# First half of the first batch in plain f32: the weights' fp16 halves made after it, in one row of tiles

## The chip, the cores and the metric

The kernel runs on one core of one Trainium2 chip. The metric is the device time of one execution in microseconds (us); the figure compared is the median of several runs. Before the change it is 1115.94 us, the median of three runs from 1112.94 to 1116.92.

The core has five engines that run their own instruction streams in order and wait for each other by semaphores: TensorE (PE in the profile, with its weight loads as PEld), VectorE (DVE), ScalarE (ACT), GpSimd (POOL) and SyncE (SP), which here only issues DMAs.

## The reference

There are 8 batches, 8 heads, 576 positions and a head width of 64. Each head is a causal attention with a decay, and its output feeds a feed-forward network (FFN) of width 2048:

```
scores = q @ k.T / sqrt(64)
cum    = cumsum(max(s, 0))
scores = where(causal, scores + min(-(cum[i] - cum[j]), 0), -1e9)
x      = softmax(scores) @ v                 # 8 heads side by side: 4608 x 512
h      = x @ w_in                            # 512 x 2048, given in float64
g      = where(h >= 1, h, where(h <= -1, 0, (h + 1)**2 / 4))
y      = g @ w_out                           # 2048 x 512, given in float64
```

The kernel computes g as min(relu(h/2 + 1/2), 1) * max(h, relu(h/2 + 1/2)), with scales by powers of two drawn in.

## The kernel before, in words

**Jobs.** The attention works in jobs: one pair of heads of one batch, and one half of its positions. The first half of a batch has 320 positions (three tiles of rows), the second 256 (two tiles, against all 576 keys). The list `jobs` runs batch by batch, first the first half of all four pairs, then the second half. A job has eight slots (`att_slot`): slots 2 to 7 hold its score units. For each unit PE makes the scores, DVE adds the mask and takes the row minimum (L418), ACT takes the exponential (L429), and POOL, ACT and DVE make fp16 halves of the normalised weights (L450 to L456). A DMA transposes these (L457). Slot 7 of the next job multiplies by V into the tile `px` (L475, `att_out`), and from `px` the job's part of X is made: a high fp16 half on ACT (L486) and a low one on DVE (L487). The first eight jobs (0 to 7, the first batch) make their scores by plain f32 matmuls (L407, tiles QF and KF), all later ones by two fp32r matmuls (L412, L413).

**FFN.** Each half batch is one FFN round of 16 steps `ft`, each for 128 of the 2048 hidden values. `ffn_h` multiplies 4 tiles of X by 128 columns of `w_in`: three fp16 products for each (high by high, high by low, low by high), so 12 matmuls for a step. ACT (L542) and DVE (L545, L546) make g in f32, and `g_split` makes its two fp16 halves on ACT (L556) and POOL (L557). `ffn_y` adds the step's share to four outputs (`m` 0 to 3) in four banks of the accumulator memory (PSUM), 3 matmuls each, so 12 again.

**Weights.** The weights arrive as float64 words, in 16 chunks of 512 KB each for `w_in` (tile `wir`) and for `w_out` (tile `wor`). `Weights.decode` makes f32 of a chunk with ACT (L198, L211) and DVE (L199, L212 to L215), and PE sums its size for a bound (L203). `Weights.scale` makes a scale from the bounds of a group of chunks. `Weights.split` then makes the fp16 halves: the high one on ACT (L228), the low one either in one DVE instruction (L236) or as a scaling (POOL L231 for `w_in`, ACT L233 for `w_out`) and a POOL subtraction (L234). For `w_in`, 11 of the 16 chunks take the DVE way, 5 the POOL way; for `w_out` all take the POOL way.

**Tiles.** 16 tiles `WI` hold the halves of `w_in`; 18 tiles `WO` first hold the f32 values of `w_in`, then the f32 values of `w_out` (two tiles further on) and then its halves. So a chunk of `w_out` can be decoded only where the chunk of `w_in` that lay there has been split.

**Order.** Jobs 0 to 3 come first, with the decoding of `w_in` between their slots; then `a_in` (a bound over all of `w_in`), `batch_scales(0)` (a dozen small DVE instructions), the first three loads of `w_out` (which wait for `a_in`) and all 16 splits of `w_in`. Then the loop over `j` begins. In `j` 0 to 15 each turn has one step of `ffn_h` for the first round and two of the tasks that decode and split `w_out`; in `j` 16 to 31 it has two steps of `ffn_y` for two of the four outputs. In these 32 turns 40 attention slots are placed, that is, jobs 4 to 8. From `j` 32 on every FFN step takes two turns, and `ffn_y` runs two steps behind `ffn_h`.

A planner then sorts the instructions of each engine. It takes them by priority (their place in the program, moved forward where `tc.high_priority` says so: `TTR_LEAD`, `FFN_LEAD`, `X_LEAD`, `W2_LEAD`) as they become ready on its own model of time. The order on each engine is fixed before the kernel runs, and on the chip each engine keeps it.

Of the kernel before, what the change touches and what calls it, by code (L numbers as in the profile page):

```python
# [22 lines left out]
P = 128  # L23
# [31 lines left out]
POOL_LO = {'wi': (8, 12, 13, 14, 15), 'wo': range(16)}  # L55
POOL_SCALE = ('wi',)
# [15 lines left out]
def attention_ffn(ctx: ExitStack, tc: tile.TileContext, qT, kT, vT, s, w_in, w_out, yT):  # L72
# [95 lines left out]
    class Weights:  # L168
        def __init__(self, name, src, held, out, tags, order, groups):
            self.name, self.src, self.held, self.out, self.tags = name, src, held, out, tags  # L170
            self.order, self.size = order, NW // groups
            self.group = {c: n // self.size for n, c in enumerate(order)}
# [18 lines left out]
        def decode(self, n):  # L191
            c, g = self.order[n], n // self.size
            raw = self.raw.pop(c)
            w = flat32(self.held[c])
            wi = w.bitcast(I32)
            lw, hw = raw[:, :, 0], raw[:, :, 1]

            A.activation(w, hw.bitcast(F32), AF.Copy, scale=2.0 ** -112)  # L198
            V.tensor_scalar(wi, wi, 3, None, ALU.logical_shift_left)  # L199

            if n % self.size == 0:
                self.sums[g] = ps_y.tile([P, 512], F32, tag=f"y{g}", name=f"sum_{self.name}{g}")
            T.matmul(  # L203
                self.sums[g][:, :NC], ones, w.bitcast(BF16).rearrange("p (n t) -> p n t", t=2)[:, :, 1],
                start=(n % self.size == 0), stop=(n % self.size == self.size - 1),
            )

            if n in self.act_low:
                dst = raw.bitcast(U16).rearrange("p n (t f) -> p n t f", f=4)[:, :, 0, 2]
                src = raw.bitcast(U8).rearrange("p n (t f) -> p n t f", f=8)[:, :, 0, 3]  # L210
                A.activation(dst, src, AF.Identity, bias=floor_bias, scale=2.0 ** -5)  # L211
# [12 lines left out]
        def split(self, n):  # L224
            c, g = self.order[n], n // self.size
            r = self.r[:, g:g + 1]
            w, hi, lo = flat32(self.held[c]), self.out[c][:, 0], self.out[c][:, 1]
            A.activation(hi, w, AF.Copy, scale=r)  # L228
            if n in self.pool_lo:
                if self.name in POOL_SCALE:  # L230
                    G.tensor_scalar(w, w, r, 1.0, ALU.mult, ALU.mult)  # L231
                else:
                    A.activation(w, w, AF.Copy, scale=r)  # L233
# [6 lines left out]
        WO, WI, ((gp, "g", G_BUFS),), [n % 4 * 4 + n // 4 for n in range(NW)], 4,  # L240
# [4 lines left out]
        WO[WO_LAG:], WO, ((ap, "raw", 2), (gp, "x0", 2), (ap, "raw", 2)), list(range(NW)), 2,  # L245
# [218 lines left out]
    def att_out(n, hf):  # L464
# [58 lines left out]
    def ffn_h(b, hf, ft):  # L523
# [4 lines left out]
        for kt in range(NKT):  # L528
            for wl, xl in ((0, 0), (0, 1), (1, 0)):
                T.matmul(  # L530
                    h[:, :N], WI[4 * kt + ft // 4][:, wl, ft % 4 * P:(ft % 4 + 1) * P], x[:, kt, xl],
# [18 lines left out]
    to_split = []  # L550

# [9 lines left out]
    def ffn_y(b, hf, ft, g, ms=tuple(range(NKT))):  # L561
# [4 lines left out]
        for m in ms:  # L566
            c0 = ft % 2 * 2 * P + m % 2 * P
            for n, (wl, gl) in enumerate(((0, 0), (1, 0), (0, 1))):
                T.matmul(  # L569
                    ys[b, hf, m][:, :N], WO[8 * (m // 2) + ft // 2][:, wl, c0:c0 + P], g[:, gl],  # L570
# [31 lines left out]
    for j in range(NPAIR):  # L602
        for k in range(8):
# [19 lines left out]
    def w2_tasks():  # L623
        for g in range(2):
            for c in range(8 * g, 8 * g + 8):
                w2.decode(c)
                w2.load(c + 3)
                yield
            w2.scale(g, TINY)
            batch_y(0, (g,))  # L630
            for c in range(8 * g, 8 * g + 8):
                w2.split(c)
                yield

    t = 8 * NPAIR
    tasks = w2_tasks()
    for j in range(16 * NP):
# [7 lines left out]
        with tc.high_priority(offset=W2_LEAD):  # L645
            for _ in range(W2_RATE):
                next(tasks, None)
        if j >= 2 * NFT:
            ffn_step(j // 2, j % 2)
        elif j < NFT:  # L650
            ffn_step(j, 0)
        else:
            if j == NFT:
                with tc.high_priority(offset=FFN_LEAD):
                    g_split()
            m = 2 * (j // 8 % 2)
            for i in range(j % 8 * 2, j % 8 * 2 + 2):
                ffn_y(*ffn_q[i], ms=(m, m + 1))
            if j == 2 * NFT - 1:
                del ffn_q[:NFT]  # L660
# [32 lines left out]
```

## Time and profile before

| | |
|---|---|
| median of three runs | 1115.94 us |
| the profiled execution: its time | 1111.73 us |
| the profiled execution: its span | 1109.9 us |
| PE busy in the span | 1010.8 us (91%) |
| DVE busy | 846.3 us (76%) |
| ACT busy | 725.8 us (65%) |
| POOL busy | 679.0 us (61%) |

All rows of the trace come from that one execution, and their times count from the span's start. Its time is 1.8 us more than its span. A row of the timeline gives start, duration (us), engine, line, operation, output and inputs, the count of merged instructions, and in brackets how long the engine had been idle before and for whom it waited. A row of the groups gives line, engine, operation, shapes and count, then busy us and mean ns of one, then the idle time before them with what ended it. A row of the windows gives a stretch, its length, then for PE, PEld, DVE, ACT and POOL the busy us with the count of instructions, and at the end the clock that was granted to TensorE (1.00 is full), the busy share of the DMA engines and GB/s. A plain f32 matmul of the program is two records in the trace (x2), each with a weight load of its own.

### The profile page before, as it was taken

Reading aid. Unit: us, or ns where it says so; the run is one execution under the profiler, and the core shown is the slowest. Engines: PE = TensorE matmul, PEld = TensorE weight load, DVE = VectorE, ACT = ScalarE, POOL = GpSimd, SP = SyncE. Lnnn points to the kernel's source line nnn. Section 1 sums busy time; section 2 is a strip of 40 time slices with the busy share of each in tenths; the row PEclk is TensorE's granted clock in tenths of the full one; section 3 lists DMA queues with packets and bytes.
Section 4 is the critical chain, followed back from the end, with each engine's and each line's share of the span. In section 5 each row is a group of like instructions: output and inputs, shape, how many; then the busy total and the mean of one; then the engine's idle time right before and its main releaser. Section 6 shows DMA issues by size and latency. Waiting matters only on the chain.

```text
span 1109.9 us, 25082 instructions
## 1 busy us (share of the span) xinstructions
PE 1010.8 (91%) x8495; PEld 774.9 (70%) x8496; DVE 846.3 (76%) x2325; ACT 725.8 (65%) x1703; POOL 679.0 (61%) x1173
## 2 busy tenths in 40 slices
PE   2456898799999999999999999899999999899998
PEld 1232466587768877777778877687778877787787
DVE  7887966688787877787778877787777887887533
ACT  4765985677567774867567765777576765777432
POOL 4782795775556764766467664666476665765522
PEclk9955999799999999999999999999999999999999
DMA  7876653786468663886468763877387763676300
GB/s 235 218 200 192 170 87 91 158 173 155 100 122 188 148 152 71 187 162 158 79 146 177 161 136 81 177 160 163 68 176 155 165 137 74 158 156 138 68 25 19
DMA packets 340775, 155.01 MB, mean 140 GB/s; under 512 B 290856, under 2 KB 322472, under 8 KB 340648
## 3 DMA queue, kind: packets, MB, share of 16 engines
q1 hardware_dynamic: 330944, 143.49, 59.6%
q10 hardware_dynamic: 9704, 9.93, 2.9%
q8 instruction: 67, 1.10, 0.4%
q14 instruction: 60, 0.49, 0.1%
HBM read 72.31 MB, written 9.73 MB: 74 GB/s over the span
## 4 chain that ended last, share of the span: by engine, by line
PE 61%; DVE 12%; POOL 8%; DMA 7%; issue 6%; ACT 5%; ACTq 0%; SPq 0%; DVEq 0%; POOLq 0%
PE y L569 25%; PE h L530 25%; PE px L475 4%; DMA pt<-pb 3%; PE s L412 3%; PE s L413 3%; DVE pb L456 2%; ACT u L542 2%; POOL pb L453 2%; POOL pb L450 2%; DVE p L418 1%; DVE Q L357 1%; DMA vt<-vb 1%; POOL vb L371 1%; DVE h L545 1%
## 5 line engine op out<-in xcount | busy, mean ns | idle before, releaser
L530 PE MATMUL h<-x,WI 128*128 128x256 f16 (+1 forms) x3072 | 463.9, 290 | 7.4 <-ACT x L486 3.4
L569 PE MATMUL y<-g,WO 128*128 128x256 f16 (+1 forms) x3072 | 457.8, 288 | 7.0 <-POOL g L557 5.3
L530 PEld LDWEIGHTS <-WI 128*128 128x128 f16 x3072 | 291.1, 99 | 97.0 <-issue 13.9
L569 PEld LDWEIGHTS <-WO 128*128 128x128 f16 x3072 | 288.1, 98 | 92.9 <-issue 13.8
L557 POOL TENSOR_TENSOR g<-u,g 128x320 f16<-128x320 f32 (+1 forms) x256 | 206.0, 805 | 152.1 <-ACT g L556 151.6
L429 ACT ACTIVATE p<-p,mn 64x64 f32<-64x64 f32 (+4 forms) x320 | 179.4, 561 | 142.7 <-DVE mn L418 122.2
L542 ACT ACTIVATE u<-h,ub,us 128x320 f32<-128x320 f32 (+1 forms) x256 | 149.1, 583 | 120.3 <-PE h L530 115.3
L545 DVE SCALAR_TENSOR_TENSOR h<-h,ws,u 128x320 f32<-128x320 f32 (+1 forms) x256 | 132.4, 517 | 110.6 <-ACT u L542 108.1
L450 POOL TENSOR_SCALAR pb<-p,rs 64x128 f16<-64x128 f32 (+4 forms) x160 | 95.3, 596 | 171.2 <-DVE rs L446 112.1
L453 POOL TENSOR_TENSOR pb<-p,pb 64x128 f16<-64x128 f32 (+4 forms) x160 | 173.9, 1087 | 9.5
L456 DVE SCALAR_TENSOR_TENSOR pb<-p,rs,pb 64x128 f16<-64x128 f32 (+4 forms) x160 | 134.6, 841 | 47.1 <-POOL pb L450 47.0
L418 DVE CUSTOM_DVE_ANT_0 p<-s,mask 64x64 f32<-64x64 f32 (+4 forms) x320 | 134.4, 420 | 31.3 <-PE s L413 23.0
L412 PE MATMUL s<-K,Q 128*64 128x64 f32 (+1 forms) x336 | 126.2, 377 | 16.0 <-DVE mn L418 10.9
L546 DVE SCALAR_TENSOR_TENSOR u<-u,r,h 128x320 f32<-128x320 f32 (+1 forms) x256 | 130.3, 509 | 6.8 <-DVE h L545 0.5
L451 ACT ACTIVATE p<-p,rs 64x64 f32<-64x64 f32 (+4 forms) x160 | 89.6, 560 | 51.3 <-DVE rs L446 49.4
L556 ACT CAST g<-u 128x320 f16<-128x320 f32 (+1 forms) x256 | 107.9, 421 | 10.3 <-DVE u L546 10.3
L413 PE MATMUL s<-K,Q 68*64 68x64 f32 (+1 forms) x336 | 102.8, 307 | 2.1 <-DMA K<-cumd 1.3
L452 POOL TENSOR_SCALAR pb<-p 64x128 f16<-64x128 f32 (+4 forms) x160 | 93.2, 583 | 11.9 <-ACT p L451 11.0
L475 PEld LDWEIGHTS <-vt 128*64 128x64 f16 x1536 | 73.4, 113 | 36.7 <-issue 30.2
L475 PE MATMUL px<-pt,vt 128*64 128x256 f16 (+3 forms) x1536 | 83.5, 259 | 13.3 <-DMA pt<-pb 8.7
L412 PEld LDWEIGHTS s<-K,Q 128*64 128x64 f32 (+1 forms) x336 | 61.5, 183 | 27.3 <-DVE mn L418 8.2
L413 PEld LDWEIGHTS s<-K,Q 68*64 68x64 f32 (+1 forms) x336 | 61.9, 184 | 5.8 <-issue 1.7
(105 smaller groups left out, 983.0 us busy)
## 6 DMA issues: line engine op xcount, KB each, us to landing
rk<-in_k_dram SPq DMA_DIRECT2D x56, 288.0 KB
v<-in_v_dram SPq DMA_DIRECT2D x32, 288.0 KB
rq<-in_q_dram SPq DMA_DIRECT2D x56, 160.0 KB
rk<-in_k_dram SPq DMA_DIRECT2D x56, 160.0 KB
wir<-in_moe_w_in_dram SPq DMA_DIRECT2D x16, 512.0 KB
wor<-in_moe_w_out_dram SPq DMA_DIRECT2D x16, 512.0 KB
rq<-in_q_dram SPq DMA_DIRECT2D x56, 128.0 KB
out_dram<-o ACTq DMA_DIRECT2D x32, 160.0 KB
```

The lines of the kernel that those rows point to most:

```text
L412: T.matmul(sc[:R, :c1 - c0], Q1[:, hd, qo:qo + R], K1[:, hd, c0:c1], start=True, stop=False)
L413: T.matmul(sc[:R, :c1 - c0], Q2[:KC, hd, qo:qo + R], K2[:KC, hd, c0:c1], start=False, stop=True)
L418: ttr[0] = V.tensor_tensor_reduce(out=Pt[:R, c0:c1], in0=sc[:R, :c1 - c0], in1=mask[:R, mo:mo + c1 - c0], scale=-0.125 if j < F32_JOBS els ...
L429: A.activation(Pt[:R, :W], Pt[:R, :W], AF.Exp, bias=m2[:R], scale=-1.0, accum_out=sums[n, i][:R, hd:hd + 1])
L453: G.tensor_tensor(los[1], pw, his[1], ALU.subtract)
L456: V.scalar_tensor_tensor(los[0], pv, rs[:R, :1], his[0], ALU.mult, ALU.subtract)
L475: T.matmul(px[hd * D:(hd + 1) * D, lo:N], VT[:, vl * NB + j, hd * D:(hd + 1) * D], PT[:, 4 * j + 2 * hd + pl, lo:], start=(m == 0), stop=( ...
L530: T.matmul(h[:, :N], WI[4 * kt + ft // 4][:, wl, ft % 4 * P:(ft % 4 + 1) * P], x[:, kt, xl], start=(n == 0), stop=(n == 3 * NKT - 1),)
L542: first = A.activation(u, h[:, :N], AF.Relu, bias=ubi[b], scale=usc[b][:, fg:fg + 1]).ins
L545: V.scalar_tensor_tensor(h[:, :N], h[:, :N], wsc[b][:, fg:fg + 1], u, ALU.mult, ALU.max)
L557: G.tensor_tensor(g[:, 1], u, g[:, 0], ALU.subtract)
L569: T.matmul(ys[b, hf, m][:, :N], WO[8 * (m // 2) + ft // 2][:, wl, c0:c0 + P], g[:, gl], start=(ft == 0 and n == 0), stop=(ft == NFT - 1 an ...
```

## The change

The first FFN round (batch 0, first half) no longer uses fp16 halves. Its X is one f32 tile (`att_out` makes it by one ACT instruction for each pair), `first_h` multiplies it by the decoded f32 values of `w_in` in plain f32 (4 matmuls for a step instead of 12), g stays in f32 (no `g_split`), and `first_y` multiplies it by the decoded f32 values of `w_out` (one matmul for each output and step instead of 3). Its scales (`us32`, `ws32`) come from the batch's scale of V alone, not from the weights' bounds; its output is copied without a scale.

All weights lie in one row of 34 tiles `WT`: the f32 values of chunk n lie two tiles behind its halves, and those of `w_out` follow those of `w_in`. So `w_out` can be decoded before `w_in` is split, and a split overwrites f32 values which the first round has used. The splits of `w_in` move from ahead of the loop to `j` 4 to 19, one for each turn; those of `w_out` to `j` 24 to 31 (chunks 0 to 7) and, with `W2_LEAD`, two for each turn in `j` 32 to 35. All of `w_out` is decoded in `j` 0 to 7. All 16 low halves of `w_in` are now made by an ACT scaling (the line of L233) and a POOL subtraction (L234); L231 and, for the weights, L236 are no longer used. `a_in`, `batch_scales(0)` and `batch_y(0)` move to `j` 16, and the first loads of `w_out` wait for the last group's bound instead of `a_in`. The 40 attention slots of these turns stay where they were.

```diff
-POOL_LO = {'wi': (8, 12, 13, 14, 15), 'wo': range(16)}
-POOL_SCALE = ('wi',)
+POOL_LO = {'wi': range(16), 'wo': range(16)}
...
-    WI = [cp.tile([P, 2, NC], F16, name=f"WI{c}") for c in range(NW)]
-    WO = [cp.tile([P, 2, NC], F16, name=f"WO{c}") for c in range(NW + WO_LAG)]
+    WT = [cp.tile([P, 2, NC], F16, name=f"WT{c}") for c in range(2 * NW + W_LAG)]
...
+            self.out, self.held = WT[base:base + NW], WT[base + W_LAG:base + W_LAG + NW]
...
             if n in self.pool_lo:
-                if self.name in POOL_SCALE:
-                    G.tensor_scalar(w, w, r, 1.0, ALU.mult, ALU.mult)
-                else:
-                    A.activation(w, w, AF.Copy, scale=r)
+                A.activation(w, w, AF.Copy, scale=r)
                 G.tensor_tensor(lo, w, hi, ALU.subtract)
...
+        if (b, hf) == (0, 0):
+            if p == 0:
+                X[b, hf] = gp.tile([P, NKT, N], F32, tag=f"x{hf}", bufs=2, name=f"x{b}_{hf}")
+            with tc.high_priority(offset=X_LEAD):
+                A.activation(X[b, hf][:, p], px[:, :N], AF.Copy, scale=e)
+            return
...
+    def first_h(ft):
+        N = HALF[0][1]
+        h = ps_h.tile([P, 512], F32, tag="h", name=f"h0_0_{ft}")
+        for kt in range(NKT):
+            T.matmul(
+                h[:, :N], flat32(w1.held[ft // 4 * NKT + kt])[:, ft % 4 * P:(ft % 4 + 1) * P], X[0, 0][:, kt],
+                start=(kt == 0), stop=(kt == NKT - 1),
+            )
+        if ft % 4 == 0:
+            g32.append(gp.tile([P, 4, N], F32, tag="g", bufs=G_BUFS, name=f"g0_0_{ft}"))
+        with tc.high_priority(offset=FFN_LEAD):
+            u = gp.tile([P, N], F32, tag="u", bufs=4, name=f"u0_0_{ft}")
+            A.activation(u, h[:, :N], AF.Relu, bias=half_bias, scale=us32)
+            V.scalar_tensor_tensor(h[:, :N], h[:, :N], ws32, u, ALU.mult, ALU.max)
+            V.scalar_tensor_tensor(g32[-1][:, ft % 4], u, 1.0, h[:, :N], ALU.min, ALU.mult)
+
+    def first_y(ft, ms):
...
+            T.matmul(
+                ys[0, 0, m][:, :N], flat32(w2.held[8 * (m // 2) + ft // 2])[:, c0:c0 + P], g32[ft // 4][:, ft % 4],
+                start=(ft == 0), stop=(ft == NFT - 1),
+            )
...
-    V.tensor_reduce(a_in, w1.bound, axis=AX, op=ALU.max)
-    batch_scales(0)
     for c in range(3):
-        w2.load(c, a_in)
-    for n in range(NW):
-        w1.split(n)
+        w2.load(c, w1.bound[:, 3:4])
     att_out(*jobs[NPAIR - 1])
...
+        if j < NW // 2:
+            with tc.high_priority(offset=W2_LEAD):
+                for c in (2 * j, 2 * j + 1):
+                    w2.decode(c)
+                    w2.load(c + 3)
+                    if c % 8 == 7:
+                        w2.scale(c // 8, TINY)
+        if j < NFT:
+            first_h(j)
+        elif j < 2 * NFT:
+            i = j - NFT
+            if i < 8:
+                for ft in (2 * i, 2 * i + 1):
+                    first_y(ft, (0, 1))
+            else:
+                for ft in range(i % 4 * 4, i % 4 * 4 + 4):
+                    first_y(ft, (i // 4,))
+        if j == NFT:
+            V.tensor_reduce(a_in, w1.bound, axis=AX, op=ALU.max)
+            batch_scales(0)
+            batch_y(0)
+        if 4 <= j < NW + 4:
+            w1.split(j - 4)
+        if NW + 8 <= j < 2 * NW:
+            w2.split(j - NW - 8)
+        elif 2 * NW <= j < 2 * NW + 4:
+            with tc.high_priority(offset=W2_LEAD):
+                for c in (8, 9):
+                    w2.split(c + (j - 2 * NW) * 2)
```

More of the change, by code (lines that the diff above doesn't have):

```diff
@@ L168, in attention_ffn, with __init__ @@
     class Weights:
-        def __init__(self, name, src, held, out, tags, order, groups):
-            self.name, self.src, self.held, self.out, self.tags = name, src, held, out, tags
+        def __init__(self, name, src, base, banks, tags, order):
+            groups = len(banks)
+            self.name, self.src, self.banks, self.tags = name, src, banks, tags
+            self.out, self.held = WT[base:base + NW], WT[base + W_LAG:base + W_LAG + NW]
             self.order, self.size = order, NW // groups
-            self.group = {c: n // self.size for n, c in enumerate(order)}
             self.bound = cp.tile([P, groups], F32, name=f"bound_{name}")
@@ L193, in decode @@
             raw = self.raw.pop(c)
-            w = flat32(self.held[c])
+            w = flat32(self.held[n])
             wi = w.bitcast(I32)
@@ L224, in split @@
         def split(self, n):
-            c, g = self.order[n], n // self.size
+            g = n // self.size
             r = self.r[:, g:g + 1]
-            w, hi, lo = flat32(self.held[c]), self.out[c][:, 0], self.out[c][:, 1]
+            w, hi, lo = flat32(self.held[n]), self.out[n][:, 0], self.out[n][:, 1]
             A.activation(hi, w, AF.Copy, scale=r)
             if n in self.pool_lo:
-                if self.name in POOL_SCALE:
-                    G.tensor_scalar(w, w, r, 1.0, ALU.mult, ALU.mult)
-                else:
-                    A.activation(w, w, AF.Copy, scale=r)
+                A.activation(w, w, AF.Copy, scale=r)
                 G.tensor_tensor(lo, w, hi, ALU.subtract)
@@ L239, in attention_ffn @@
         "wi", lambda c: w_in[c // 4 * P:(c // 4 + 1) * P, c % 4 * NC:(c % 4 + 1) * NC, :],
-        WO, WI, ((gp, "g", G_BUFS),), [n % 4 * 4 + n // 4 for n in range(NW)], 4,
+        0, (0, 1, 2, 3), ((gp, "g", G_BUFS),), [n % 4 * 4 + n // 4 for n in range(NW)],
     )
@@ L244, in attention_ffn @@
         .rearrange("(j p) n t -> p j n t", p=P),
-        WO[WO_LAG:], WO, ((ap, "raw", 2), (gp, "x0", 2), (ap, "raw", 2)), list(range(NW)), 2,
+        NW, (2, 3), ((ap, "raw", 2), (gp, "x0", 2), (ap, "raw", 2)), list(range(NW)),
     )
@@ L480, in att_out @@
                 )
+        e = exs[b][:, p:p + 1]
+        if (b, hf) == (0, 0):
[4 more added lines that the diff above has]
+            return
         if p == 0:
@@ L550, in attention_ffn, with first_scales @@
     to_split = []
+    g32 = []
+    us32, ws32 = (cp.tile([P, 1], F32, name=n) for n in ("us32", "ws32"))
+    def first_scales():
+        V.tensor_scalar(us32, msc[0], 2.0 ** -13, None, ALU.mult)
+        V.tensor_scalar(ws32, msc[0], 2.0 ** -12, None, ALU.mult)
+    def first_h(ft):
[14 more added lines that the diff above has]
+    def first_y(ft, ms):
+        N = HALF[0][1]
+        for m in ms:
+            if ft == 0:
+                ys[0, 0, m] = ps_y.tile([P, 512], F32, tag=f"y{m}", name=f"y0_0_{m}")
+            c0 = ft % 2 * 2 * P + m % 2 * P
+            T.matmul(
+                ys[0, 0, m][:, :N], flat32(w2.held[8 * (m // 2) + ft // 2])[:, c0:c0 + P], g32[ft // 4][:, ft % 4],
+                start=(ft == 0), stop=(ft == NFT - 1),
+            )
+            if ft == NFT - 1:
+                o = gp.tile([P, N], F32, tag="o", bufs=O_BUFS, name=f"o0_0_{m}")
+                with tc.high_priority(offset=FFN_LEAD):
+                    A.copy(o, ys[0, 0, m][:, :N])
+                nc.scalar.dma_start(yT[m * P:(m + 1) * P, :N], o)
     def g_split(first=None):
@@ L612, in attention_ffn @@
                 batch_scales_v(0)
+    first_scales()
     while late:
         late.pop(0)()
-    V.tensor_reduce(a_in, w1.bound, axis=AX, op=ALU.max)
-    batch_scales(0)
     for c in range(3):
-        w2.load(c, a_in)
-    for n in range(NW):
-        w1.split(n)
+        w2.load(c, w1.bound[:, 3:4])
     att_out(*jobs[NPAIR - 1])
[L623 to L633, printed above, removed]
     t = 8 * NPAIR
-    tasks = w2_tasks()
     for j in range(16 * NP):
@@ L644, in attention_ffn @@
             t += 1
-        with tc.high_priority(offset=W2_LEAD):
-            for _ in range(W2_RATE):
-                next(tasks, None)
+        if j < NW // 2:
[27 more added lines that the diff above has]
+                    w2.split(c + (j - 2 * NW) * 2)
         if j >= 2 * NFT:
             ffn_step(j // 2, j % 2)
[L650 to L660, printed above, removed]
     with tc.high_priority(offset=FFN_LEAD):
```

11 lines of the change are left out of this document (6 added, 5 removed).

## The prediction

> **What bounds the kernel now.** I read the windows first, cut where the first FFN round begins and ends, to see which engine is full in which stage.
>
> ```profile
> span 1109.9 us, 25082 instructions
> ```
>
> ```profile
> 55.00:104.00 49.00, 25.93 (x104) 13.42 (x105) 38.69 (x105) 28.48 (x60) 31.54 (x53) 0.53 0.78 206
> 104.00:112.00 8.00, 8.00 (x24) 3.98 (x23) 7.22 (x23) 5.70 (x10) 0.79 (x1) 0.50 0.39 118
> 112.00:140.00 28.00, 23.14 (x136) 14.08 (x136) 25.58 (x53) 26.30 (x51) 21.77 (x25) 0.93 0.68 168
> 140.00:187.00 47.00, 46.81 (x346) 32.02 (x342) 30.54 (x92) 30.61 (x62) 33.64 (x43) 1.00 0.48 89
> 187.00:212.00 25.00, 14.08 (x114) 11.01 (x115) 16.16 (x53) 15.22 (x43) 17.66 (x32) 0.73 0.74 150
> 212.00:1000.00 788.00, 766.41 (x6798) 606.65 (x6797) 630.12 (x1775) 538.34 (x1314) 497.24 (x909) 0.99 0.66 142
> ```
>
> From 212 on PE is busy 766 of 788 us at full clock: it is the bound, and its work there is untouched by the change. So the end moves by as much as the moment moves at which PE enters that stage. Before it PE is starved until 104 (clock 0.53), full from 140 to 187, and starved again from 187 to 212. Next I looked in the timeline for what opens the two starved stretches.
>
> ```profile
> 83.67 1.15 POOL L234 TENSOR_TENSOR WI<-WO,WI 128x512 f16<-128x512 f32 x1
> ```
>
> ```profile
> 102.99 0.51 ACT L486 ACTIVATE x<-px,ex 128x320 f16<-128x320 f32 x1
> 103.54 0.55 DVE L487 SCALAR_TENSOR_TENSOR x<-px,ex,x 128x320 f16<-128x320 f32 x1
> ```
>
> The last half of `w_in` is ready at 84.8, the last part of the first X only at 104. So the first round does not wait for the split that the change takes from its path; it waits for the attention of job 3. What the split cost there is engine time ahead of that job. The second stretch:
>
> ```profile
> 183.93 1.25 PE L569 MATMUL y<-g,WO 128*128 128x320 f16 x8
> ...
> 186.10 0.65 PE L407 MATMUL s<-KF,QF 68*128 68x288 f32 x2
> ```
>
> ```profile
> 194.91 4.69 SPq L457 DMA_TRANSPOSE pt<-pb  x2
> ...
> 200.62 2.77 PE L475 MATMUL px<-pt,vt 128*64 128x256 f16 x30 [4.49 <-DMA pt<-pb]
> ...
> 208.28 2.72 PE L530 MATMUL h<-x,WI 128*128 128x256 f16 x12 [0.81 <-DVE u L546]
> ```
>
> PE finishes the first round's y at 185, and only then makes the last scores of job 7. Softmax, transposes and `px` of that job take until 203, and the second round runs freely from 208. PE stood in its fixed order: y work that could have covered this latency had been spent ahead of it.
>
> **PE's own cost.** Full clock, matmuls back to back:
>
> ```profile
> 144.35 1.79 PE L530 MATMUL h<-x,WI 128*128 128x320 f16 x12
> 145.98 0.92 PE L407 MATMUL s<-KF,QF 68*128 68x448 f32 x2
> 146.73 1.79 PE L530 MATMUL h<-x,WI 128*128 128x320 f16 x12
> ```
>
> Twelve fp16 matmuls of 320 columns take from 144.35 to 145.98: 1.63 us, 0.136 each. One plain f32 matmul of 448 columns (two records) takes from 145.98 to 146.73: 0.75 us, so 320 columns take 0.75 x 320/448 = 0.536 us. The round had 192 + 192 fp16 matmuls, 52.2 us; it gets 64 + 64 f32 ones, 68.6 us. PE pays 16.4 us more. This row is the same kind of instruction on 68 rows instead of 128; I take no other price for it, and keep its weight loads for the rivals.
>
> **What the other engines gain and lose.**
>
> ```profile
> L236 DVE SCALAR_TENSOR_TENSOR WI<-WO,r_wi,WI 128x512 f16<-128x512 f32 x11 | 9.5, 883 | 0.0
> L234 POOL TENSOR_TENSOR WI<-WO,WI 128x512 f16<-128x512 f32 x5 | 6.2, 1244 | 0.0
> L231 POOL TENSOR_SCALAR WO<-WO,r_wi 128x512 f32<-128x512 f32 x5 | 4.4, 883 | 0.1
> L228 ACT ACTIVATE WI<-WO,r_wi 128x512 f16<-128x512 f32 x16 | 10.3, 707 | 0.0
> L233 ACT ACTIVATE WO<-WO,r_wo 128x512 f32<-128x512 f32 x16 | 11.5, 719 | 0.1
> L487 DVE SCALAR_TENSOR_TENSOR x<-px,ex,x 128x320 f16<-128x320 f32 x8 | 4.3, 538 | 0.4 <-ACT x L486 0.4
> L556 ACT CAST g<-u 128x320 f16<-128x320 f32 x31 | 14.0, 451 | 5.0 <-DVE u L546 5.0
> L557 POOL TENSOR_TENSOR g<-u,g 128x320 f16<-128x320 f32 x31 | 28.1, 907 | 31.6 <-ACT g L556 31.5
> ```
>
> DVE loses 11 low halves (9.5 us) and 4 low parts of X (4 x 0.538 = 2.2). ACT loses 16 casts of g (16 x 0.451 = 7.2) and gains 16 scalings (16 x 0.719 = 11.5): 4.3 more. POOL loses 16 subtractions of g (14.5) and the old w_in work (6.2 + 4.4), and gets 16 subtractions (16 x 1.244 = 19.9): 5.2 less. Where they fall matters more. All of the w_in split leaves the stretch before 104: 9.5 us of DVE, 10.3 of ACT, 10.6 of POOL. `batch_scales(0)` leaves it too, a dozen small DVE instructions, from
>
> ```profile
> 73.05 0.20 DVE L282 TENSOR_SCALAR r<-mb,a_in 128x1 f32<-128x1 f32 x1
> ...
> 77.44 0.20 DVE L298 TENSOR_SCALAR gb<-gb 128x1 f32<-128x1 f32 x1
> ```
>
> a stretch of 4.6 us that they share with attention; I count 3. At `j` 16 nothing of the first round is behind it: its scales serve the second round. The output is copied by as many ACT instructions and DMAs as before. The SP queue carries the same 16 loads of `w_out`; they come some 2 us earlier and still stand between the transposes. One more piece leaves with the split:
>
> ```profile
> 80.19 2.72 POOL L234 TENSOR_TENSOR WI<-WO,WI 128x512 f16<-128x512 f32 x2
> ```
>
> ```profile
> 81.83 3.73 DVE L199 TENSOR_SCALAR WO<-WO 128x512 int32<-128x512 int32 x2
> ...
> 103.12 0.43 DVE L199 TENSOR_SCALAR WO<-WO 128x512 int32<-128x512 int32 x1 [0.87 <-ACT WO L198]
> ```
>
> Beside a POOL subtraction two shifts of DVE take 3.73 us, alone 0.43 each: 2.9 us lost. The Trainium skill says in "GPSIMD Engine Reference", section Key points, that GpSimd shares its SBUF interfaces with VectorE and contends with its instructions in a two-port mode or with two SBUF inputs. The trace agrees with it here, and by that rule the 11 further subtractions that the change gives POOL would hold DVE up again, later.
>
> **The sum.** First, when X is ready. Ahead of 104 DVE is relieved of 9.5 + 3 + 2.9 + three low parts of X (1.6) = 17 us, and it was busy 38.69 of 49 us there. The upper bound of the gain is these 17 us. The lower bound is nothing: the stretch also holds waits that the change leaves, for the loads of `w_out`, whose decoding stands ahead of attention on ACT and DVE.
>
> ```profile
> 98.13 0.71 ACT L198 ACTIVATE WO<-wor 128x512 f32<-128x512 f32 x1 [3.40 <-DMA wor<-in_moe_w_out_dram]
> ```
>
> I take 10, a little over the middle since DVE was nearly four fifths busy: X at 94.
>
> Second, PE's work from there to its full stage. From 104 to 212, scaled by the clock, it did 8.00 x 0.50 + 23.14 x 0.93 + 46.81 + 14.08 x 0.73 = 82.6 us; with the f32 price that is 99.0.
>
> Third, what it loses. 108 - 82.6 = 25.4 us were lost: 4.0 to the half clock at first, 6.5 from 112 to 140 (28 - 23.14 x 0.93), 0.2, and 14.7 from 187 to 212 (25 - 14.08 x 0.73). The first 4.0 stay, since PE is still starved until X. The 6.5 go: they were h steps waiting for the chain through ACT and DVE, and an f32 step gives that chain 2.14 us instead of 1.63. Of the 14.7, I take half to go. PE has 34 us of y to put over job 7 instead of 26, and the splits of `w_out`, which had gone ahead of attention on ACT by `W2_LEAD` in `j` 0 to 15, come behind it; against that, y may again be used up first. The value between nothing and 14.7 is a choice. Left: 4.0 + 7 = 11.
>
> PE enters its full stage at 94 + 99 + 11 = 204 instead of 212: 8 us earlier. Made against the profiled execution, 1111.7 - 8 = 1103.7. That execution lies 4.2 us below the median of the runs, 1115.9; on the median the forecast is 1108. Its own range, with 5 to 13 us for the start and 4 to 18 lost, is 1098 to 1120.
>
> **Rivals.**
> *The start is hidden anyway* (chance 0.25). X waits for job 3's transposes and for the decoding of `w_out` paced by its DMA, and stays near 104 (the 3.40 us wait speaks for it, the DVE's 38.69 of 49 against). Then 104 + 99 + 11 = 214: 2 us later, 1118.
>
> *The gap at the end of the round stays and ACT lengthens it* (0.20; slower). ACT must now split all of `w_in` inside the round and chunks 8 to 15 of `w_out` with raised priority in `j` 32 to 35: 8 x (0.707 + 0.719) = 11.4 us, where the second round's X and u stand too. ACT was busy 15.22 of 25 us from 187 to 212; with 11.4 more it would be full. If these splits are placed ahead of job 7's exponentials and X, half of it, 6 us, falls on the path, and no part of the 25.4 is won: 94 + 99 + 25.4 + 6 = 224, 12 us later, 1128. It decides from the point where the first of these splits stands before the last L486 of the second X; behind it the price is nothing. For it speaks the raised priority, against it that the second round's y needs these halves only two steps on and PE has h to do.
>
> *The subtractions on POOL hold up DVE* (0.04). The 16 shifts of `w_out`'s decoding fall near them; at 1.4 us lost for each (3.73/2 - 0.43) and half of them met, 11 us come back: 3 us later, 1119. DVE's 25.58 of 28 us from 112 to 140 speaks for it; against it, decoding has priority and should mostly be over before `j` 4.
>
> *Weight loads in f32 are not hidden* (0.03).
>
> ```profile
> 145.84 0.33 PEld L407 LDWEIGHTS s<-KF,QF 68*128 68x128 f32 x2
> ```
>
> The two loads of an f32 matmul take 0.33 us. Exposed, 128 x 0.33 = 42 us are added to the 8 won: 34 later, 1150. Against it: the loads begin at 145.84 and end inside the 0.75 us of their matmul, which was not lengthened. The Trainium skill says in "TensorE: Matmul & The Clock Gate", section Weight-path perf modes, that the fast weight load is not used for FP32 operands, which speaks against the change; the row shows slower loads, but covered.
>
> *All gaps but the cold clock go* (0.06): 94 + 99 + 4 = 197, 15 earlier, 1101.
>
> **How the numbers follow.** The likeliest case, 0.42, gives 1108. The range of 8 in 10 reaches to the early case's far side and to the slower rival: 1095 to 1128. About 0.5%, 5.6 us, is what a measurement of this kernel can tell from no change. Of the 0.42, 0.38 lies below 1110.4 and 0.04 within; the early case adds 0.06 and the hidden start 0.02: faster 0.46. Same: 0.04 + 0.22 of the hidden start + 0.03 of POOL + 0.03 of the second rival with a small price = 0.32. Slower: the rest, 0.22.
>
> **What would show it.** Right: the last L486 of the first X near 94; the first round's f32 matmuls following each other at 0.54 us; the last first-round y near 195; no stretch of over 8 us with PE under half busy before the second round; from there to the end the same length as before. Wrong at the start: L486 at 102 or later. Wrong at the gap: `px` of job 7 over 12 us behind the last y. Wrong altogether: a different length from the second round to the end, since I take that stage as unchanged.

## The result, and the profile after

The change makes the kernel slower: 1121.81 us (median of 10 runs, 1119.59 to 1124.89) against 1113.79 us for the kernel before (10 runs, 1110.12 to 1116.92), a ratio of 1.0076 with a 95% interval of 1.0059 to 1.0093. That is about 8 us more, where 8 less were forecast.

The profiled execution of the changed kernel has a span of 1117.8 us, 7.9 more than before. First, whether the loss lies ahead of PE's full stage or in it. The timeline of PE gives the same two steps in both kernels: `px` of job 8 and of the last job. Before:

```profile
213.13 0.80 PE L475 MATMUL px<-pt,vt 128*64 128x320 f16 x16
...
1047.39 1.51 PE L475 MATMUL px<-pt,vt 128*64 128x256 f16 x30
```

After:

```profile
220.11 0.80 PE L473 MATMUL px<-pt,vt 128*64 128x320 f16 x16
...
1055.09 1.51 PE L473 MATMUL px<-pt,vt 128*64 128x256 f16 x30
```

The changed kernel is 7.0 us behind at the first of them and 7.7 at the last. So nearly the whole loss has been made by 220, and the 830 us behind it cost the same as before within 0.7. The windows of the changed kernel, cut at its own stages (the columns are those of the prediction's windows):

```profile
55.00:86.60 31.60, 20.74 (x88) 11.82 (x86) 19.59 (x71) 16.93 (x38) 14.33 (x36) 0.94 0.95 227
86.60:104.00 17.40, 17.33 (x59) 11.42 (x59) 11.86 (x32) 10.41 (x20) 5.25 (x7) 0.92 0.58 132
104.00:122.00 18.00, 12.07 (x33) 6.94 (x32) 12.50 (x32) 12.43 (x23) 7.35 (x8) 0.81 0.51 133
122.00:184.00 62.00, 61.59 (x274) 41.43 (x274) 40.46 (x90) 49.58 (x87) 40.06 (x45) 1.00 0.49 116
184.00:220.00 36.00, 19.80 (x138) 14.40 (x135) 27.12 (x79) 25.86 (x62) 27.70 (x43) 0.67 0.54 117
```

The round now starts at 86.6, has a hole from 104 to 122, is full until 184, and then PE is starved for 36 us, where it was 25 before. The timeline of ACT and PE in the changed kernel, for the start and for the price of one f32 matmul:

```profile
86.13 0.52 ACT L484 ACTIVATE x<-px,ex 128x320 f32<-128x320 f32 x1
```

```profile
91.32 2.31 PE L566 MATMUL h<-x,WT 128*128 128x320 f32 x8
93.47 1.24 PE L584 MATMUL y<-g,WT 128*128 128x320 f32 x4
```

X is complete at 86.65. The eight records (four matmuls) of an h step take from 91.32 to 93.47: 2.15 us, 0.54 each. Then the end of the round, in the timeline of PE:

```profile
181.66 2.05 PE L584 MATMUL y<-g,WT 128*128 128x320 f32 x7
...
185.46 0.16 PE L114 MATMUL col_m<-t_m,ones 1*128 1x1 bf16 x1 [0.33 <-DVE t_m L112]
185.55 1.24 PE L405 MATMUL s<-KF,QF 68*128 68x288 f32 x4
...
205.35 2.77 PE L473 MATMUL px<-pt,vt 128*64 128x256 f16 x30 [5.39 <-DMA pt<-pb]
...
214.60 2.72 PE L534 MATMUL h<-x,WT 128*128 128x256 f16 x12 [0.47 <-DVE u L550]
```

The last y ends at 183.7, 1.5 us earlier than before (185.2). But from there to `px` of job 7 it is now 21.6 us instead of 15.4, so `px` comes 4.7 us later (205.35 against 200.62), and the second round runs freely 6.3 us later (214.60 against 208.28). What stands in between is seen on ACT and on POOL. ACT in the changed kernel, up to the exponential for the scores that PE finished at 186.8:

```profile
186.67 0.70 ACT L229 ACTIVATE WT<-WT,r_wo 128x512 f16<-128x512 f32 x1
187.41 0.72 ACT L231 ACTIVATE WT<-WT,r_wo 128x512 f32<-128x512 f32 x1
...
188.67 0.71 ACT L229 ACTIVATE WT<-WT,r_wo 128x512 f16<-128x512 f32 x1
...
189.89 0.77 ACT L427 ACTIVATE p<-p,mn 128x576 f32<-128x576 f32 x1
```

The same exponential in the kernel before, where PE finished these scores at 186.75 and no split stands on ACT:

```profile
188.05 0.77 ACT L429 ACTIVATE p<-p,mn 128x576 f32<-128x576 f32 x1
```

POOL in the changed kernel, for the halves of job 7's weights (L448, L450, L451), with two subtractions of `w_out` (L232) among them:

```profile
192.19 0.80 POOL L448 TENSOR_SCALAR pb<-p,rs 128x640 f16<-128x640 f32 x1 [0.60 <-DVE rs L444]
192.96 1.16 POOL L232 TENSOR_TENSOR WT<-WT,WT 128x512 f16<-128x512 f32 x1
194.09 1.29 POOL L450 TENSOR_SCALAR pb<-p 128x640 f16<-128x640 f32 x1
...
195.43 1.16 POOL L232 TENSOR_TENSOR WT<-WT,WT 128x512 f16<-128x512 f32 x1
196.55 1.91 POOL L451 TENSOR_TENSOR pb<-p,pb 128x640 f16<-128x640 f32 x1
```

The first and the last of these halves in the kernel before:

```profile
190.11 0.80 POOL L450 TENSOR_SCALAR pb<-p,rs 128x640 f16<-128x640 f32 x1 [0.33 <-DVE rs L446]
...
192.59 2.18 POOL L453 TENSOR_TENSOR pb<-p,pb 128x640 f16<-128x640 f32 x1
```

The DMA that transposes them was issued at 194.91 in the kernel before (shown in the prediction), and in the changed kernel, in the timeline of SP, at 199.38:

```profile
199.38 3.60 SPq L455 DMA_TRANSPOSE pt<-pb  x1
```

So the changed kernel falls behind step by step: the scores end at the same time, the exponential starts 1.8 us later, the last half on POOL ends 3.7 us later (198.46 against 194.77), the DMA is issued 4.5 us later, and `px` follows 4.7 us later.

Over the 36 us from 184 to 220 no engine is full (DVE 27.12, ACT 25.86, POOL 27.70), but on ACT and POOL instructions of this chain find a split ahead of them. The groups of two stretches say where the splits of `w_out` lie. Before, from 104 to 184, all 16 of them:

```profile
L234 POOL TENSOR_TENSOR WO<-WO,WO 128x512 f16<-128x512 f32 x16 | 20.0, 1250 | 2.1 <-ACT WO L233 1.7 <-POOL WO L234 0.5
```

After, from 184 to 212:

```profile
L232 POOL TENSOR_TENSOR WT<-WT,WT 128x512 f16<-128x512 f32 x8 | 9.2, 1158 | 0.7 <-PE s L405 0.5 <-POOL WT L232 0.2
L231 ACT ACTIVATE WT<-WT,r_wo 128x512 f32<-128x512 f32 x7 | 5.0, 715 | 0.1
L229 ACT ACTIVATE WT<-WT,r_wo 128x512 f16<-128x512 f32 x7 | 5.0, 711 | 0.1
```

### The profile page after: what moved, and what is told of

Read it like the earlier page. It is cut to its first block, busy times and chain, and to the rows that moved or that the text cites. A ratio compares the mean times of both kernels' runs of the same rounds, so it can differ in the third digit from the quotient of the medians.

```text
span 1117.8 us, 24800 instructions
## 1 busy us (share of the span) xinstructions
PE 1024.0 (92%) x8366; PEld 787.3 (70%) x8368; DVE 836.8 (75%) x2313; ACT 731.0 (65%) x1703; POOL 667.6 (60%) x1163
## 4 chain that ended last, share of the span: by engine, by line
PE 55%; DVE 14%; POOL 9%; DMA 8%; ACT 7%; issue 6%; ACTq 0%; SPq 0%; DVEq 0%; POOLq 0%
PE h L534 23%; PE y L611 22%; PE px L473 3%; DMA pt<-pb 3%; PE s L410 3%; DVE pb L454 3%; PE s L411 3%; DMA wor<-in_moe_w_out_dram 2%; POOL pb L448 2%; POOL pb L451 2%; DVE p L416 2%; ACT p L427 2%; ACT u L546 2%; DVE Q L355 1%; DVE h L549 1%
## 5 line engine op out<-in xcount | busy, mean ns | idle before, releaser
L611 PE MATMUL y<-g,WT 128*128 128x256 f16 (+1 forms) x2880 | 427.5, 287 | 8.9 <-POOL g L599 6.9
L534 PE MATMUL h<-x,WT 128*128 128x256 f16 (+1 forms) x2880 | 428.6, 287 | 2.8 <-DVE x L491 2.1
L611 PEld LDWEIGHTS <-WT 128*128 128x128 f16 x2880 | 269.1, 98 | 84.1 <-issue 13.9
L534 PEld LDWEIGHTS <-WT 128*128 128x128 f16 x2880 | 270.6, 98 | 78.4 <-issue 6.0
L599 POOL TENSOR_TENSOR g<-u,g 128x256 f16<-128x256 f32 (+1 forms) x240 | 189.6, 790 | 134.0 <-ACT g L598 133.1
L448 POOL TENSOR_SCALAR pb<-p,rs 64x128 f16<-64x128 f32 (+4 forms) x160 | 97.5, 610 | 213.6 <-DVE rs L444 140.7
L546 ACT ACTIVATE u<-h,ub,us 128x256 f32<-128x256 f32 (+1 forms) x240 | 139.4, 581 | 123.7 <-PE h L534 114.9
L549 DVE SCALAR_TENSOR_TENSOR h<-h,ws,u 128x256 f32<-128x256 f32 (+1 forms) x240 | 123.8, 516 | 102.3 <-ACT u L546 99.8
L451 POOL TENSOR_TENSOR pb<-p,pb 64x128 f16<-64x128 f32 (+4 forms) x160 | 172.8, 1080 | 9.5
L454 DVE SCALAR_TENSOR_TENSOR pb<-p,rs,pb 64x128 f16<-64x128 f32 (+4 forms) x160 | 139.0, 869 | 48.0 <-POOL pb L448 47.9
L410 PE MATMUL s<-K,Q 128*64 128x64 f32 (+1 forms) x336 | 126.9, 379 | 17.4 <-DVE mn L416 10.3
L550 DVE SCALAR_TENSOR_TENSOR u<-u,r,h 128x256 f32<-128x256 f32 (+1 forms) x240 | 121.8, 507 | 6.6 <-DVE h L549 0.5
L598 ACT CAST g<-u 128x256 f16<-128x256 f32 (+1 forms) x240 | 100.7, 419 | 5.9 <-DVE u L550 5.9
L450 POOL TENSOR_SCALAR pb<-p 64x128 f16<-64x128 f32 (+4 forms) x160 | 91.4, 571 | 15.2 <-ACT p L449 14.0
```

Source lines behind the costliest of these rows:

```text
L410: T.matmul(sc[:R, :c1 - c0], Q1[:, hd, qo:qo + R], K1[:, hd, c0:c1], start=True, stop=False)
L451: G.tensor_tensor(los[1], pw, his[1], ALU.subtract)
L454: V.scalar_tensor_tensor(los[0], pv, rs[:R, :1], his[0], ALU.mult, ALU.subtract)
L534: T.matmul(h[:, :N], w1.out[ft // 4 * NKT + kt][:, wl, ft % 4 * P:(ft % 4 + 1) * P], x[:, kt, xl], start=(n == 0), stop=(n == 3 * NKT - 1),)
L546: first = A.activation(u, h[:, :N], AF.Relu, bias=ubi[b], scale=usc[b][:, fg:fg + 1]).ins
L549: V.scalar_tensor_tensor(h[:, :N], h[:, :N], wsc[b][:, fg:fg + 1], u, ALU.mult, ALU.max)
```

## The experiments

Three theories stood at the start. *A, crowding*: the splits of `w_out`, which the change puts behind the first round, stand ahead of job 7's softmax on ACT and POOL. *B, order*: PE has spent all y before the scores of job 7 that y could have covered. *C, price*: the f32 matmuls cost PE 16 us, and that is the loss. The runs are told by theory. Gains "against after" are differences of the medians; each ratio is to executions of the kernel before that were taken together with the run.

**A, the low halves of `w_out` taken away or moved to another engine.** The first run leaves out the low halves of `w_out` (it sets them to zero), the second those of both weights; the third makes those of `w_out` by one DVE instruction each instead of ACT and POOL.

```diff
             if n in self.pool_lo:
+                if self.name == "wo":          # second run: both weights
+                    G.memset(lo, 0.0)
+                    return
                 A.activation(w, w, AF.Copy, scale=r)
...
-POOL_LO = {'wi': range(16), 'wo': range(16)}
+POOL_LO = {'wi': range(16), 'wo': ()}          # third run
```

> Start: the changed kernel, 8.0 us above the kernel before. Leaves out the low halves of w_out: each is set to zero by POOL instead of an ACT scaling and a POOL subtraction, which takes 11.5 us from ACT and most of 19.8 us from POOL between 168 and 201 us and gives DVE nothing. Theory A (crowding): 5 to 9 us less, px of job 7 near 201. Theory B (order): at most 3 us less.

> Start: the changed kernel, 8.0 us above the kernel before. Leaves out the low halves of w_in and of w_out (zero, set by POOL), so 23 us leave ACT and most of 39 us leave POOL between 98 and 201 us. If the splits of w_in, moved into the first round, hold it up, this is at least 4 us less than the run that leaves out those of w_out alone. Theory B (order): within 2 us of that run.

> Start: the changed kernel, 8.0 us above the kernel before. Only edit: the low halves of w_out are made by one DVE instruction each, so 16 scalings leave ACT (11.5 us) and 16 subtractions leave POOL (some 19.8 us), most of them between 168 and 201 us. Theory A (crowding: the splits of w_out on ACT and POOL run through job 7's softmax and X and lengthen the gap before the second round): 5 to 8 us less than the changed kernel, so 0 to 3 us above the kernel before, and px of job 7 at 201 or earlier instead of 205. Theory B (order: PE has spent all y of the first round ahead of job 7's last scores, the gap is that job's latency): at most 2 us less. Theory C (price: PE's 16.4 us more are simply added): no change.

Without the low halves of `w_out`: 1112.13 us, ratio 0.9983 (0.9963 to 1.0002). That is 9.7 us less than after, a little more than A expected, and the whole loss. The gap is back to where it was before, with `px` of job 7 and the free h steps 1 us ahead of before:

```profile
199.64 2.77 PE L476 MATMUL px<-pt,vt 128*64 128x256 f16 x30 [3.73 <-DMA pt<-pb]
...
207.21 2.72 PE L537 MATMUL h<-x,WT 128*128 128x256 f16 x12 [0.47 <-DVE u L553]
```

With both weights' low halves zero: 1111.39 us, ratio 0.9975 (0.9955 to 0.9996), no different. The windows of the two runs show why. First with the low halves of `w_out` alone left out:

```profile
104.00:122.00 18.00, 12.39 (x34) 7.29 (x34) 13.11 (x35) 12.49 (x23) 7.36 (x8) 0.81 0.53 132
122.00:184.00 62.00, 61.93 (x277) 41.85 (x277) 39.84 (x90) 47.66 (x84) 38.68 (x53) 1.00 0.49 116
```

Then with those of both weights left out:

```profile
104.00:122.00 18.00, 17.59 (x61) 10.72 (x61) 13.77 (x41) 12.92 (x22) 8.85 (x14) 1.00 0.76 184
122.00:184.00 62.00, 58.62 (x258) 39.79 (x257) 33.32 (x87) 37.48 (x68) 24.11 (x43) 0.94 0.44 103
```

The hole from 104 to 122 is gone (PE 17.59 us at full clock, against 12.39 at 0.81), so PE did 7.6 us of work more there, scaled by the clock. But from 122 to 184 it did 6.8 us less (58.62 x 0.94 against 61.93). It waited again between 128 and 139, and the first of these waits leads back to ACT, where the decoding of `w_out` waited for its load:

```profile
128.18 0.66 ACT L199 ACTIVATE WT<-wor 128x512 f32<-128x512 f32 x1 [3.92 <-DMA wor<-in_moe_w_out_dram]
```

By 184 both runs had done the same work, 87.7 and 87.8 us from 86.6 on. So filling the hole gained nothing: PE lost the same time again right behind it. The last y of the first run:

```profile
176.85 6.62 PE L587 MATMUL y<-g,WT 128*128 128x320 f32 x24
```

The last y and `px` of job 7 in the second:

```profile
177.86 5.01 PE L586 MATMUL y<-g,WT 128*128 128x320 f32 x18
...
199.08 2.77 PE L475 MATMUL px<-pt,vt 128*64 128x256 f16 x30 [3.56 <-DVE pb L456]
```

In both, `px` comes 16.2 us behind the end of the last y, against 15.4 in the kernel before and 21.6 in the changed one.

With one DVE instruction for each low half: 1118.44 us, ratio 1.0049 (1.0026 to 1.0073), 3.4 less than after, where A expected 5 to 8 and `px` of job 7 at 201 or earlier. `px` now waits for an instruction of job 7's softmax on DVE, so the crowd seems to have gone there:

```profile
204.97 2.77 PE L473 MATMUL px<-pt,vt 128*64 128x256 f16 x30 [3.85 <-DVE rs L443]
```

**A, the splits of `w_out` moved in time.** One run writes all 16 at `j` 32 to 39 without raised priority; another gives all 16 the raised priority, four for each turn in `j` 32 to 35, but makes their scale from the last half of job 7's weights, so that the data holds them back until job 7 has left ACT and POOL.

```diff
-        if NW + 8 <= j < 2 * NW:
-            w2.split(j - NW - 8)
-        elif 2 * NW <= j < 2 * NW + 4:
-            with tc.high_priority(offset=W2_LEAD):
-                for c in (8, 9):
-                    w2.split(c + (j - 2 * NW) * 2)
+        if 2 * NW <= j < 2 * NW + 8:           # first run
+            for c in (0, 1):
+                w2.split(c + (j - 2 * NW) * 2)
...
+            for g in range(2):                 # second run; lo: job 7's last low half
+                V.scalar_tensor_tensor(rx[:R, g:g + 1], lo[:, 0, :1], 0.0, w2.r[:R, g:g + 1], ALU.mult, ALU.add)
+            w2.r = rx
```

> Start: the changed kernel, 8.0 us above the kernel before. Only edit: all 16 splits of w_out are placed in j 32 to 39 in the program's order and without raised priority, so that they stand behind job 7's exponentials and X on ACT. Theory A (crowding): 4 to 8 us less than the changed kernel, if the second round's y does not then wait for the halves. Theory B (order): at most 2 us less. Theory C (price): no change.

> The changed kernel with all 16 splits of w_out held back by data until job 7's last subtraction of its weights' low halves (their scale is made from it), which ends at 198.46 in the trace of after. Theory A (the splits crowd job 7's softmax, and that is the loss): px of job 7 comes at 195 to 200 instead of 205.35, and the time falls by 6 to 10 us against after, to 1112 to 1116. Rival (the crowding only moves: the second round's y waits for the halves, since 16 x 1.43 us of ACT and 16 x 1.24 us of POOL now stand between 192 and 222): px earlier all the same, but PE enters its full stage at 218 or later, time 1119 or more.

The first gave 1119.04 us, ratio 1.0051 (1.0029 to 1.0073), 2.8 less than after where A expected 4 to 8. But 15 of the 16 splits stood on ACT between 170 and 200 all the same, so this run says little about A. The second gave 1128.16 us (4 runs), ratio 1.0135 (1.0084 to 1.0186): slower still. Its rows show both halves of what happened:

```profile
199.45 2.77 PE L477 MATMUL px<-pt,vt 128*64 128x256 f16 x30 [3.30 <-DMA pt<-pb]
...
230.90 2.72 PE L538 MATMUL h<-x,WT 128*128 128x256 f16 x12 [2.41 <-DVE u L554]
```

```profile
208.00:220.00 12.00, 9.29 (x70) 6.87 (x68) 11.37 (x20) 10.00 (x22) 11.31 (x19) 0.76 0.41 86
```

Out of the way, the splits let `px` of job 7 come at 199.45, 15.8 us behind the last y (183.69), as without their low halves. So crowding is what delayed it. But behind job 7 they crowd the second round and jobs 8 and 9: DVE is busy 11.37 of 12 us, and PE waits 2.41 us for u. A expected 1112 to 1116 and missed; the rival, that the crowding only moves, is right. In neither of the two places tried, around job 7 and behind it, were these 20 us of POOL and 23 of ACT free. The kernel before had them inside the first round, between 104 and 184; what they cost it there, no run shows.

**B, the order on PE.** The scores of job 7's last unit stand behind all y because the scale of batch 1's V (the tiles `row_m` and `col_m`, L104 and L114, the latter at 185.46 in the rows above) uses the two PSUM banks of the score tiles and waits for reductions on DVE. One run gives these two tiles the banks of h, in the changed kernel, another in the kernel before. A third places 32 of the 40 attention slots in the first 16 turns of the changed kernel, and a fourth does both in the kernel before.

```diff
-        row = ps_s.tile([P, 512], F32, tag="s", name=f"row_{name}")
+        row = (ps_h.tile([P, 512], F32, tag="h", name=f"row_{name}") if name == "m1"
+               else ps_s.tile([P, 512], F32, tag="s", name=f"row_{name}"))
...
-        for _ in range(1 + (j % 4 == 3 if j < 2 * NFT else j % 8 == 3 and j < 6 * NFT)):
+        for _ in range(2 if j < NFT else j % 2 if j < 2 * NFT else 1 + (j % 8 == 3 and j < 6 * NFT)):
```

> Start: the changed kernel, 8.0 us above the kernel before. Only edit: the two small PE products of batch_scales_v(1) (row_m, col_m) write to the two banks of the h tiles instead of the two banks of the score tiles, so that job 7's last two pairs of score units need not wait for the chain of DVE reductions between them; in PE's order part of the last y then stand behind these scores. Theory B (order: the gap is job 7's latency behind its last scores, and these stand behind all y): 6 to 12 us less than the changed kernel, px of job 7 near 196 instead of 205. Theory A (crowding by the splits of w_out): at most 3 us less. Theory C (price): no change.

> Start: the kernel before. Only edit: the same as in the run with the changed kernel, row_m and col_m of batch 1 in the banks of the h tiles. In PE's order 80 of the 192 y matmuls then stand behind job 7's scores instead of none. Theory B (order): the gap of 25 us before the second round shrinks by half or more, 8 to 14 us below the kernel before. Theories A and C say nothing of it: no change.

> Start: the changed kernel, 8.0 us above the kernel before. Only edit: of the 40 attention slots of j 0 to 31, 32 stand in j 0 to 15 (two for each turn) and 8 in j 16 to 31, so that jobs 4 to 7 come before the first round's y in the program. Theory B (order): y now covers job 7's latency, 5 to 12 us less. Theory A (crowding): within 2 us. Theory C (price): no change.

> The kernel before with the edit of e7 and that of e4 (32 of the 40 attention slots in the first 16 turns). If attention of job 7 is still late relative to y in e7: another 2 to 5 us below e7's 1107.55, 1102 to 1106. If the first half of the round, where ACT and DVE are already full, pays for the earlier slots: 1107 or more.

Banks, changed kernel: 1119.64 us, ratio 1.0048 (1.0030 to 1.0066), 2.2 less than after, where B expected 6 to 12. Only two matmuls of y came to stand behind job 7's last scores there (1.24 us), and `px` came at 202.68, not near 196. Slots, changed kernel: 1116.58 us, ratio 1.0035 (1.0016 to 1.0054), 5.2 less, inside B's 5 to 12 but not by B's way: all y still stands ahead of job 7's last scores, it ends 2.0 us earlier (181.67), and `px` comes 20.6 us behind it, at 202.24. Banks, kernel before: 1107.55 us, ratio 0.9945 (0.9926 to 0.9964), 6 us faster than before and the fastest kernel here that computes in full; 8 to 14 were expected. There y does stand behind job 7's last scores (177.34), and PE waits only 0.25 us right ahead of `px`:

```profile
192.00:200.00 8.00, 4.32 (x53) 3.51 (x53) 4.09 (x17) 4.97 (x14) 5.31 (x13) 1.00 0.81 162
```

```profile
193.83 1.51 PE L477 MATMUL px<-pt,vt 128*64 128x256 f16 x30 [0.25 <-DVE mn L420]
```

`px` comes at 193.83 instead of 200.62. Part of the gap stays (PE is busy 4.32 of 8 us from 192 to 200), and the second round runs freely from 204.06 instead of 208.28. Both edits in the kernel before give 1109.22 us, ratio 0.9958 (0.9939 to 0.9978): nothing beyond the banks alone. So order is a real part of the gap, but one that both kernels have; it doesn't explain their difference. The slots alone were not tried in the kernel before.

**A and B together.** The splits held behind job 7, with the banks:

> The edit of e10 and that of e6 (the two small matmuls of batch 1's scale in other PSUM banks) together. If crowding and order are separate parts of the gap, the gains add: 3 to 6 us below e10, 1107 to 1112, level with before or a little below. If both only shorten the same wait, the time is that of e10 within 1.5 us.

1127.41 us (4 runs), ratio 1.0140 (1.0099 to 1.0180), the same as without the banks, and not the 1107 to 1112 of gains that add. With the second round crowded, the better order ahead of it bought nothing.

**C, the price on PE.** The first round reads only the upper 16 bits of its f32 tiles, as bf16; this leaves out the lower bits of X, g and the weights in that round. In the trace each of its matmuls is one record instead of two, and four of them take 0.57 us (from 137.91 to 138.48) instead of 2.15.

```diff
-                h[:, :N], flat32(w1.held[ft // 4 * NKT + kt])[:, ft % 4 * P:(ft % 4 + 1) * P], X[0, 0][:, kt],
+                h[:, :N], top16(flat32(w1.held[ft // 4 * NKT + kt])[:, ft % 4 * P:(ft % 4 + 1) * P]), top16(X[0, 0][:, kt]),
```

> Start: the changed kernel, 8.0 us above the kernel before. Only edit: the first round's 128 matmuls read the upper 16 bits of their f32 operands as bf16, so the round is computed with less precision and PE needs about a quarter of its time: 68.6 us become some 17. Theory C (price): at least the 16.4 us are won, 8 or more below the kernel before. Theory B (order): the y stand ahead of job 7's last scores with 34 us; without most of it these come earlier, 8 to 20 us less. Theory A (crowding): ACT was busy 49.6 of 62 us there and sets the pace, so 0 to 5 us less; the gap on PE only becomes wider.

1104.33 us, ratio 0.9925 (0.9902 to 0.9947), 17.5 less than after. About 51 us were taken from PE (128 x 0.536 less 128 x 0.14), and a third of them was won. The last y and `px` of job 7:

```profile
155.11 1.22 PE L587 MATMUL y<-g,WT 128*128 128x320 bf16 x4 [3.99 <-DVE g L579]
...
178.62 2.77 PE L476 MATMUL px<-pt,vt 128*64 128x256 f16 x30 [5.40 <-DMA pt<-pb]
```

The last y ends at 156.3, 27 us earlier than after and not 51: inside the round PE now waits for g (3.99 us in the first of these rows), and DVE was busy 16.90 and ACT 16.27 of the 18 us from 104 to 122. From the last y to `px` it takes 22.3 us, about as long as after (21.6), so `px` is 27 us earlier as well. Another 9 us are lost behind it.

## Why the prediction was wrong, by its own steps

**First step, when X is ready: right in kind, too small.** Forecast 94, with a gain of 10 between 0 and 17; it came at 86.65, a gain of 17.4. That is about all that DVE was relieved of, the upper bound; from 55 to 86.6 DVE is now busy 19.59 of 31.60 us. ACT and POOL were relieved there too, and no run separates the three. The rival "the start is hidden anyway" is out.

**Second step, PE's own work: right.** 99.0 us forecast. Scaled by the clock, PE did 17.33 x 0.92 + 12.07 x 0.81 + 61.59 + 19.80 x 0.67 = 100.6 us from 86.6 to 220. The price of 0.536 us for a matmul, taken from a row with 68 contraction rows, was met with 0.54 on 128. The weight loads stayed hidden, so that rival is out as well. For the rule cited with it (the Trainium skill, "TensorE: Matmul & The Clock Gate", section Weight-path perf modes) the trace shows no cost here: an f32 load of the h steps takes 0.21 us in the mean against 0.10 for an fp16 one, under matmuls that are slower still (two records in 0.54 us against one in 0.136).

**Third step, the time PE loses: this one failed.** Forecast 11 us, of which 4.0 at the cold start and 7 in the gap at the end. Measured: 133.4 - 100.6 = 32.8, of which 0.4 from 122 to 184.

- At the start 1.5 us from 86.6 to 104 (17.40 - 17.33 x 0.92), as the clock was 0.92 and not 0.5.
- From 104 to 122, 8.2 us (18.00 - 12.07 x 0.81), where "the 6.5 go" was forecast. PE waited for a row minimum of attention on DVE, which had, among other work, 2.6 us of the decoding of `w_out` in front of it (timeline of PE):

```profile
115.16 1.33 PE L405 MATMUL s<-KF,QF 68*128 68x288 f32 x2 [4.63 <-DVE mn L416]
```

The prediction read the 6.5 as h steps waiting for ACT and DVE. In the kernel before, PE's longest waits from 112 to 140 were 2.27 us for u, which are of that kind, but also 1.59 and 0.87 us for row minima of attention, which a longer h step doesn't relieve.

- At the end 22.7 us (36.00 - 19.80 x 0.67), where half of 14.7 was to go.

86.6 + 100.6 + 32.8 = 220, against 212 before. The earlier start (17.4) paid for the f32 price (16.4 forecast, and the last y came 1.5 us earlier than before), and the gap then gave the 8 us of the result.

The slower rival described the end: "The gap at the end of the round stays and ACT lengthens it". Its place and its direction were right, its price (6 us) near the 8.0 by which the gap grew (22.7 against 14.7). It named eight splits, and about that many stood in the gap: seven pairs on ACT and eight subtractions on POOL from 184 to 212. Two things in it were not right. It named ACT alone; POOL's subtractions stood between the halves of job 7's weights as well. And its argument against itself, that y of the second round needs the halves only two steps on, was of no use, since held back they cost more (1128.16 us). I gave it 0.20.

Underneath lies how the gap was costed: as 14.7 us of lost time, of which half would go, because PE had more y "to put over job 7" and because the splits of `w_out` "come behind" the attention. Neither happened. PE's order puts all y ahead of job 7's last scores, so no y lay over the gap, and the splits stood on ACT and POOL inside it. From those scores to `px` runs a chain of DVE, ACT, POOL and a DMA. The time from the end of the last y to `px` went with what stood in that chain, and not with when PE came to it: 15.4 us before, 16.2 in both runs with low halves at zero, 15.8 with the splits held back, but 21.6 after and 22.3 with the round in bf16, where y ended 27 us earlier. So this term should have been a chain: last scores, then every instruction up to `px` with what stands ahead of it on each engine.

The signs named in the prediction: X near 94, wrong in value, right in sense; 0.54, seen; last y near 195, it was 183.7; no stretch of over 8 us under half busy, broken at the end of the round; `px` of job 7 over 12 us behind the last y, which was named as the sign of a wrong gap, with 21.6; the same length from the second round to the end, seen within 0.7 us.

## What to carry to other kernels

When work is moved out of a stretch that waits, ask which stretch receives it and whether that one has a latency chain with nothing on the bound engine to cover it; there, moved instructions of 0.7 or 1.2 us are paid for though no engine's average is near full: here 10.0 us on ACT and 9.2 on POOL made the time from the last y to `px` 6.2 us longer. Cost the gap ahead of a full stage as a chain from its last producer to its first consumer, not as a share of lost time that shrinks. A hole ahead of it is worth filling only as far as the next limit: 7.6 us of work done earlier gained nothing where PE waited again right behind the hole. And look at what the in-order engine spends ahead of such a chain: two small tiles in other banks won 6 us in the kernel before.

## What was not expected of the hardware

Decoding on DVE beside subtractions on POOL slows down by half. Groups of DVE from 86 to 160, in the changed kernel and in the run without any subtraction for the weights:

```profile
L215 DVE SCALAR_TENSOR_TENSOR WT<-wor,WT 128x512 int32<-128x512 int32 x7 | 7.3, 1041 | 0.0
```

```profile
L215 DVE SCALAR_TENSOR_TENSOR WT<-wor,WT 128x512 int32<-128x512 int32 x7 | 4.9, 701 | 1.2 <-PE sum_wo L204 1.2
```

1.04 us against 0.70 for the same instruction. That is the effect which the prediction cited from "GPSIMD Engine Reference" and placed among the rivals at 0.04. It is there, as that page of the Trainium skill says. With those for `w_out` gone, the subtractions for `w_in` cost nothing at the end, since leaving them out as well changed nothing (1111.39 against 1112.13 us). Nor is it on the chain to `px` of job 7 in the changed kernel: DVE's own low half of the weights ended at 194.79 (L454), POOL's at 198.46. Whether it adds to the 1.6 us by which the second round falls back further behind `px` is open. The hole from 104 to 122 isn't explained by it alone: in the run with the splits held behind job 7 the same instruction took 1.04 us too, and PE, which came there later, was busy 15.87 of the 18 us. A stronger case stands in that run, in the timelines of DVE and of POOL:

```profile
224.25 0.61 DVE L458 SCALAR_TENSOR_TENSOR pb<-p,rs,pb 128x384 f16<-128x384 f32 x1
...
226.89 3.57 DVE L458 SCALAR_TENSOR_TENSOR pb<-p,rs,pb 64x128 f16<-64x128 f32 x1 [0.63 <-POOL pb L450]
```

```profile
229.16 1.15 POOL L232 TENSOR_TENSOR WT<-WT,WT 128x512 f16<-128x512 f32 x1
```

An instruction of 128 columns took 3.57 us, one of 384 columns of the same line 0.61. It ended at 230.46, as POOL's subtraction ended (230.31), the last of several that POOL ran one after another from 227.39 on. That the one waited for the other is argued from the times, not shown by a run of its own.
